# Splitting one weight load and reordering two value loads in a fused attention and SwiGLU kernel

## Chip, cores and metric

The kernel runs on one core of one Trainium2 chip. The metric is the device time of one execution in microseconds (us). A core has five engines that run beside each other and wait for one another by semaphores: PE (TensorE, the matmuls), DVE (VectorE), ACT (ScalarE), POOL (GpSimd) and SP (SyncE, which only starts transfers here). PEld is PE's weight load. Transfers started by POOL, by SP and by ACT share the core's 16 DMA engines.

## What is computed

Attention without a mask over 8 batches, 12 heads, 448 tokens and head size 64, then a SwiGLU block over all 3584 tokens. Inputs and output are float32; the kernel computes in float16 with float32 sums.

```python
scores = (q @ k.T) / sqrt(64)                  # per batch and head, 448 x 448
attn   = softmax(scores)
x      = (attn @ v) -> [3584, 768]             # heads side by side
out    = (silu(x @ w_gate) * (x @ w_val)) @ w_out   # 768 -> 1536 -> 768
```

## The kernel before

**Pairs.** Two heads form a pair; there are 48 pairs, numbered 0 to 47, six to a batch. `q` and `k` of a pair are loaded by POOL with a cast to float16 into `qkraw`, brought into the order for a transpose, and turned so that the head dimension lies on the partitions (`qkT`). From pair 11 on POOL copies them into `qk` (L237 and L260) and SP starts a DMA transpose in two halves (L239 and L243 from pair 12 on). PE multiplies keys by queries (`qk_quad`: L329 for a pair's own three chunks, L341 for a rest chunk, tile `s`), ACT takes the exponential into `E` (L349), and PE multiplies `E` by the values (`pv_*`, L420, tile `acc`). DVE normalizes into `xt` (L449 and L450). The rest chunk is shared: an even pair from 12 (QUAD) on and the odd one behind it put their last 64 keys of each head together, so L341 needs the `qkT` of both pairs.

**Values.** `load_v` asks for the values of a pair: one transfer below pair 12, two of 64 KB each (`load_keys`, L177) from pair 12 on. They land in `vraw`, and DVE copies them (`copy_v`, L218) into `vo`, which L420 reads.

**Weights.** `load_w` loads a quarter of the gate or value weights in two transfers, or one half (384 of the 768 output columns) of the output weights `wo` in one transfer (L231, 1152 KB in float16). The second half of the columns is `wo[1]`. `plain_out` multiplies 12 row blocks `fb` of `hts` by the 12 row blocks of `wo[oh]` in turn (L650, tile `op`). The differences of `wo` for later products (`out_sums`, L529 to L532) run on DVE and read both.

**Order.** Each engine executes its instructions in the order in which the program emits them (`manual_schedule`). The loop over `plan` emits one visit after another. In a visit stand, in this order: two or three chunks of scores, the opening of a value product (`pv_open`, `pv_rest`), the preparation of pairs `pr` whose first chunk is entered (`prep`, then `load_qk16` of pair `pr + 6`, then `load_v` of pair `pr + 3`), the rest of the value product with its normalization, `copy_v` of the pair that comes next, the weights that `wq` lists for `pr`, and a share of the feed-forward work (`run_o` for L650 with its DVE sums, `run_pair` for two gate and value blocks: L557, L584, L610, L616). So POOL's queue holds, around the change:

- entering pair 8: copies of pair 11, queries and keys of 14 (three transfers: one of queries, two of keys), `wo[1]`
- entering pair 9: copies of pairs 12 and 13, queries and keys of 15, values of 12
- entering pair 10: copies of pair 14, queries and keys of 16, values of 13
- entering pair 11: copies of pair 15, queries and keys of 17, values of 14
- entering pair 12: copies of pair 16, queries and keys of 18, values of 15, and so on

PSUM tiles that matter: `acc`, `vp` and `op` come from a pool of two banks (`ps_f`); `s` and `gp` from a pool of three double banks (`ps_s`). A matmul that starts a tile waits until the earlier tile in that bank has been read.

Of the kernel before, what the change touches and what calls it, by code (L numbers as in the profile page):

```python
# [18 lines left out]
GP = 3  # L19
# [13 lines left out]
QUAD = 12  # L33
# [31 lines left out]
def kernel(  # L65
# [10 lines left out]
    nc = tc.nc  # L76
# [6 lines left out]
    NFB = DF // 128  # L83
    NHP = H // 2
    NPAIR = B * NHP
# [3 lines left out]
    OH = DM // 2  # L89
# [47 lines left out]
    NH = NFB // 2  # L137
# [16 lines left out]
    wo = [wo_all[:, i] for i in range(2)]  # L154
# [17 lines left out]
    def load_keys(eng, dst, src, h0, n):  # L172
        for s in range(2):
            rows = bass.AP(
                src.tensor, (h0 * S + s * KR) * D, [[(2 * NC - 1) * D, 64], [S * D, n], [1, NC * D]]
            )
            eng.dma_start(dst[ts(s, 64)], rows)  # L177
# [8 lines left out]
    def load_qk16(pr, n=2):  # L186
        for t, src in ((0, q), (1, k)):
            if pr >= QUAD and t:
                if n == 1:
                    kd = rawslot(pr)[:, 1].rearrange("p (h x) -> p h x", h=2)  # L190
                else:
                    kd = raws_all[:, pr % RS // 2, 1].rearrange("p b (h x) -> p (b h) x", h=2)
                load_keys(nc.gpsimd, kd, k, 2 * pr, 2 * n)
                continue
            flat = src.rearrange("b h s d -> (b h) s d")[2 * pr : 2 * pr + 2 * n]
            if n == 1:
                dst = rawslot(pr)[0:P, t].rearrange("p (h x) -> p h x", h=2)
            else:
                dst = raws_all[0:P, pr % RS // 2, t].rearrange("p b (h x) -> p (b h) x", h=2)
            nc.gpsimd.dma_start(dst, flat.rearrange("h (p c) d -> p h (c d)", c=NC))  # L200
        for p in range(pr, pr + n):
            v4 = rawslot(p).rearrange("p t (h c d) -> p t h c d", h=2, c=NC)
            raw[p] = (v4[0:P, 0], v4[:, 1] if p >= QUAD else v4[0:P, 1])

    def load_v(pr, n=1):
        b, h = divmod(2 * pr, H)
        if pr >= QUAD:
            vd = vraw[:, ds(pr % VS, n)].rearrange("p r h c d -> p (r h) (c d)")
            load_keys(nc.gpsimd, vd, v, 2 * pr, 2 * n)
            return  # L210
        nc.gpsimd.dma_start(
            vraw[0:P, ds(pr % VS, n)].rearrange("p r h c d -> p (r h) (c d)"),
            v[b, h : h + 2 * n].rearrange("h (p c) d -> p h (c d)", c=NC),
        )
# [2 lines left out]
        m = 128 if pr >= QUAD else P  # L217
        nc.vector.tensor_copy(Vts[pr % NV][0:m, :, :, 0:D], vraw[0:m, pr % VS])  # L218

    def load_w(kind, i):  # L220
        if kind == "o":
            src = moe_w_out[:, ts(i, OH)].rearrange("(f p) m -> p f m", p=128)
            dst = wo[i]
        else:
            src = (moe_w_gate if kind == "g" else moe_w_val)[:, ts(i, DF // 4)].rearrange(
                "(t a p) m -> t p a m", p=128, t=2
            )
            for t in range(2):
                nc.gpsimd.dma_start(wgv[kind, i][:, ts(t, NCB // 2), :], src[t])
            return  # L230
        nc.gpsimd.dma_start(dst[:], src)  # L231

    def prep_quad(pr):
        rq, rk = raw[pr]
        qk16 = attp.tile([128, 2, NC, 2, D], FP16, tag="qk16", name="qk16", bufs=3)
        for dst, src in ((qk16[:, 0], rk), (qk16[0:P, 1], rq)):
            nc.gpsimd.tensor_copy(dst.rearrange("p c h d -> p h c d"), src)  # L237
        qkT[pr] = attp.tile([128, NC * 128 + S], FP16, tag="qkT", name="qkT", bufs=QB)
        nc.sync.dma_start_transpose(  # L239
            qkT[pr][:, 0 : NC * 128].rearrange("p (c q) -> p c q", q=128),  # L240
            qk16[:, 0].rearrange("p c h d -> p (c h d)"),
        )
        nc.sync.dma_start_transpose(  # L243
            qkT[pr][:, NC * 128 :].rearrange("p (c q) -> p c q", q=P),
            qk16[0:P, 1].rearrange("p c h d -> p (c h d)"),
        )

    def prep(pr):
        if pr >= QUAD:
            return prep_quad(pr)  # L250
        rq, rk = raw[pr]
        if pr == 0 or pr >= NPE:
            qk16 = attp.tile([128, 2, NC, 2, D], FP16, tag="qk16", name="qk16", bufs=3)[0:P]
            for t, src in enumerate((rq, rk)):
                dst = qk16[:, 1 - t].rearrange("p c h d -> p h c d")
                if pr == 0:
                    nc.vector.tensor_copy(dst[:, 0], src[:, 0])
                    nc.scalar.activation(dst[:, 1], src[:, 1], AF.Copy)
                else:
                    nc.gpsimd.tensor_copy(dst, src)  # L260
        qkT[pr] = attp.tile([128, 2 * S + D], FP16, tag="qkT", name="qkT", bufs=QB)
        if pr >= NPE:
            nc.sync.dma_start_transpose(
                qkT[pr][:, 0 : 2 * S].rearrange("p (c q) -> p c q", q=P),
                qk16.rearrange("p t c h d -> p (t c h d)"),
            )
            nc.sync.dma_start_transpose(
                qkT[pr][:, 2 * S :].rearrange("p (c q) -> p c q", c=1),
                qk16[0:D, 1, 0].rearrange("p h d -> p (h d)"),
            )  # L270
            return None

        def turn0():
            for t in range(2):
                tp = ps_s.tile([128, 2, 512], FP32, tag="s", name="tp")
                for c in range(NC):
                    for hx in range(2):
                        nc.tensor.matmul(
                            tp[ts(hx, 64), c // 2, ds(c % 2 * P, P)],
                            lhsT=qk16[:, 1 - t, c, hx],  # L280
                            rhs=ident[0:P, 0:P],
                            start=True,
                            stop=True,
                        )
                dst = qkT[pr][:, ts(1 - t, S)].rearrange("p (a x) -> p a x", a=2)
                copies = [nc.vector.tensor_copy(dst[:, 0], tp[:, 0, 0 : 2 * P])]
                if t == 0:
                    copies.append(nc.vector.tensor_copy(qkT[pr][:, 2 * S :], tp[:, 0, 0:D]))
                other = nc.scalar.activation(dst[:, 1], tp[:, 1, 0 : 2 * P], AF.Copy)
                for copy in copies:  # L290
                    tc.declare_no_dep(other.ins, copy.ins, reason="another bank, other columns")

        def turn():
            if pr < WIDE + 2:
                tp = ps_s.tile([128, 2, 1024], FP16, tag="s", name="tp")[:, 0]
            else:
                tp = ps_f.tile([128, 1024], FP16, tag="f", name="tp")
            for i in range(2 * NC + 1):
                t, c = (1 - i // NC, i % NC) if i < 2 * NC else (0, 0)
                for hx in range(2):  # L300
                    src = raw[pr][t][:, hx, c, :]
                    nc.tensor.transpose(tp[ts(hx, 64), ts(i, P)], src, ident[0:P, 0:P])  # L302
            nc.vector.tensor_copy(qkT[pr][:], tp[:, 0 : 2 * S + D])

        return turn if pr else turn0
# [585 lines left out]
    with tc.manual_schedule():  # L891
# [6 lines left out]
        for vo in Vts:  # L898
# [14 lines left out]

        wq = {
            0: [("qk", 6), ("g", 0), ("v", 0)],
            1: [("V", 2), ("qk", 8, 1), ("g", 1), ("v", 1)],
            3: [("qk", 9, 1), ("qk", 10), ("g", 2), ("v", 2)],
            4: [("g", 3), ("v", 3), ("qk", 12)],
            6: [("V", 3), ("o", 0)],
            8: [("o", 1)],  # L920
        }

        def emit(item):
            if item[0] == "qk":
                load_qk16(*item[1:])
            elif item[0] == "V":
                load_v(item[1] * GP, GP)
            else:
                load_w(*item)

# [233 lines left out]
        g = FIRST * NC  # L1164
# [36 lines left out]
        for x, (chunks, todo) in enumerate(plan):  # L1201
# [23 lines left out]
            for pr in entered:  # L1225
                lead = [pr + 3] if pr + 3 < QUAD else [pr + 3, pr + 4] if pr + 3 == QUAD else [pr + 4]
                for p in lead:
                    if NPE <= p < NPAIR:
                        prep(p)
                if 14 <= pr + LA < NPAIR:  # L1230
                    load_qk16(pr + LA, 1)
                if 12 <= pr + 3 < NPAIR:
                    load_v(pr + 3)
            for pr, c in chunks:
                if c == 2 and pr < NPE - 2:
# [13 lines left out]
            for pr in entered:  # L1249
                for w in wq.pop(pr, []):  # L1250
                    emit(w)
# [204 lines left out]
```

## Time and profile before

| | |
|---|---|
| median of 3 runs | 428.99 us (428.96 to 429.71) |
| profiled execution, its own time | 429.37 us |
| its span, first to last instruction | 427.6 us |
| mean granted TensorE clock | 0.998 |
| DVE busy | 270.1 us (63%) |
| ACT busy | 245.1 us (57%) |
| POOL busy | 232.3 us (54%) |
| transfers started by POOL | 24.56 MB |
| transfers started by SP | 24.47 MB |

Times in the timeline count from the start of the span. A line of it gives start, duration, engine, source line, operation, tiles (written first, read behind the arrow), the number of instructions merged into it and, in square brackets, how long the engine sat idle before it and what ended that. Starting a transfer takes POOL 0.6 to 1.0 us; the transfer then lands later, and the view of transfers tells after how long. A matmul's end is modelled, so neighbouring lines of PE overlap a little.

### The profile page before, as it was taken

The page shows a single profiled execution, that of the slowest core. Times are in us where ns is not written, and L with a number is a line of the kernel's source. Part 1 is how long each engine was busy: PE and PEld are TensorE (multiplying, and loading weights), DVE is VectorE, ACT ScalarE, POOL GpSimd, SP SyncE. Part 2 cuts the span into 40 slices and gives each one's busy share as a digit, 9 for nine tenths or more (in the row PEclk, how much of TensorE's full clock was granted, in tenths as well). Part 3 has the DMA queues.
Part 4 walks back from the last instruction along what each step waited for, and adds up shares of the span by engine and source line. Part 5 has one row for each costly group of instructions (what it writes and reads, how often), then busy time and mean ns, then how long its engine had stood idle before and what let it go on. Part 6 is the DMA issues. An engine that isn't in the chain of part 4 may idle for free.

```text
span 427.6 us, 11629 instructions
## 1 busy us (share of the span) xinstructions
PE 420.1 (98%) x4636; PEld 289.8 (68%) x4636; DVE 270.1 (63%) x643; ACT 245.1 (57%) x395; POOL 232.3 (54%) x353
## 2 busy tenths in 40 slices
PE   8999999999999999999999999999999999999996
PEld 3666656555556777747666677777888995555795
DVE  4666562676669665575545776667777765565663
ACT  6975667546656655546667546568655235545221
POOL 8655633999778683649653785935999000000000
PEclk9999999999999999999999999999999999999999
DMA  9999999999999999999989996823100331000125
GB/s 139 181 200 200 199 174 188 137 159 218 138 136 122 137 159 135 127 153 134 126 147 122 149 151 106 145 45 97 25 1 18 97 102 48 0 0 2 38 76 148
DMA packets 108951, 50.02 MB, mean 117 GB/s; under 512 B 60896, under 2 KB 105696, under 8 KB 108896
## 3 DMA queue, kind: packets, MB, share of 16 engines
q0 software_dynamic: 46800, 24.56, 49.6%
q1 hardware_dynamic: 61776, 24.47, 34.7%
q8 instruction: 36, 0.59, 0.6%
q10 hardware_dynamic: 320, 0.25, 0.2%
q14 instruction: 19, 0.16, 0.2%
HBM read 49.55 MB, written 11.01 MB: 142 GB/s over the span
## 4 chain that ended last, share of the span: by engine, by line
PE 89%; DVE 3%; ACT 3%; DMA 2%; issue 1%; POOL 1%; SPq 0%; ACTq 0%; DVEq 0%; POOLq 0%
PE og L679 17%; PE gp L557 17%; PE vp L557 12%; PE un L802 10%; PE ub L802 8%; PE acc L420 8%; PE s L329 5%; PE op L650 3%; PE acc L385 2%; PE s L359 2%; DMA qkT<-qk 1%; ACT E L367 1%; PE s L341 1%; PE tp L302 1%; DVE t L610 1%; PE wp L163 1%
## 5 line engine op out<-in xcount | busy, mean ns | idle before, releaser
L349 ACT ACTIVATE E<-s 128x896 f16<-128x896 f32 x126 | 106.6, 918 | 40.5 <-PE s L329 28.5
L557 PE MATMUL gp<-X,wg 128*128 128x384 f16 (+1 forms) x360 | 73.9, 347 | 0.0
L237 POOL COPY qk<-qkraw 128x512 f16<-128x512 f16 x72 | 45.2, 668 | 51.4 <-DMA qkT<-qk 50.6
L557 PE MATMUL vp<-X,wv 128*128 128x384 f16 (+3 forms) x360 | 66.7, 321 | 0.2
L610 DVE SCALAR_TENSOR_TENSOR t<-sg,gp 128x384 f32<-128x384 f32 (+1 forms) x60 | 36.3, 607 | 41.4 <-ACT sg L584 41.2
L557 PEld LDWEIGHTS <-wv 128*128 128x128 f16 x462 | 43.7, 98 | 26.2 <-DVE xt L450 0.5
L557 PEld LDWEIGHTS <-wg 128*128 128x128 f16 x360 | 32.8, 98 | 26.3 <-issue 2.1
L177 POOL DMA_DIRECT2D vraw<-in_v_dram x72 | 43.8, 627 | 11.5 <-DVE hts L616 7.6
L584 ACT ACTIVATE sg<-gp 128x384 f32<-128x384 f32 (+1 forms) x60 | 32.1, 537 | 28.1 <-PE gp L557 27.4
L177 POOL DMA_DIRECT2D qkraw<-in_k_dram x70 | 42.3, 616 | 6.8 <-DMA wo<-in_moe_w_out_dram 5.1
L367 ACT ACTIVATE E<-s 112x896 f16<-112x896 f32 x48 | 40.6, 917 | 8.4 <-PE s L359 8.3
L420 PEld LDWEIGHTS <-E 128*128 128x128 f16 (+1 forms) x1152 | 37.4, 96 | 11.2 <-issue 4.7
L679 PEld LDWEIGHTS <-hts 128*128 128x128 f16 x528 | 44.1, 98 | 0.3
L420 PE MATMUL acc<-vo,E 128*128 128x65 f16 (+1 forms) x1152 | 42.3, 192 | 0.9 <-DVE X L492 0.3
L616 DVE SCALAR_TENSOR_TENSOR hts<-t,vp 128x384 f16<-128x384 f32 (+3 forms) x60 | 32.5, 541 | 5.4 <-PE vp L557 1.9
L704 ACT ACTIVATE osb<-og 128x384 f32<-128x384 f32 x21 | 10.3, 491 | 38.1 <-PE og L679 38.1
L450 DVE TENSOR_TENSOR xt<-acc,R 128x256 f16<-128x256 f32 x72 | 30.6, 425 | 2.5
L200 POOL DMA_DIRECT2D qkraw<-in_q_dram x43 | 29.3, 681 | 4.0 <-DMA vraw<-in_v_dram 0.9
L329 PE MATMUL s<-qkT 64*128 64x448 f16 x216 | 30.2, 354 | 0.2
L679 PE MATMUL og<-wo,hts 128*128 128x192 f16 x264 | 29.0, 246 | 0.0
L679 PEld LDWEIGHTS <-hsum 128*128 128x128 f16 x300 | 25.5, 98 | 1.2 <-DVE og L728 0.3
L449 DVE RECIPROCAL R<-acc 128x4 f32<-128x4 f32 x72 | 12.7, 177 | 18.6 <-PE acc L420 18.4
(181 smaller groups left out, 713.8 us busy)
## 6 DMA issues: line engine op xcount, KB each, us to landing
vraw<-in_v_dram POOLq DMA_DIRECT2D x72, 64.0 KB, 4.5
qkraw<-in_q_dram POOLq DMA_DIRECT2D x39, 112.0 KB, 4.4
qkraw<-in_k_dram POOLq DMA_DIRECT2D x68, 64.0 KB, 4.4
wg<-in_moe_w_gate_dram POOLq DMA_DIRECT2D x8, 288.0 KB, 10.1
wv<-in_moe_w_val_dram POOLq DMA_DIRECT2D x8, 288.0 KB, 10.7
wo<-in_moe_w_out_dram POOLq DMA_DIRECT2D x2, 1152.0 KB, 19.5
out_dram<-osb SPq DMA_DIRECT2D x7, 288.0 KB, 3.8
out_dram<-osb SPq DMA_DIRECT2D x6, 336.0 KB, 3.2
```

What stands on the lines that cost most here:

```text
L177: eng.dma_start(dst[ts(s, 64)], rows)
L237: nc.gpsimd.tensor_copy(dst.rearrange("p c h d -> p h c d"), src)
L329: nc.tensor.matmul(s[:, hx, 0:S], lhsT=t[ts(hx, 64), ts(c + low(pr, hx), 128)], rhs=t[ts(hx, 64), ds(NC * 128, S)], start=True, stop=True,)
L349: nc.scalar.activation(e[:, 0 : 2 * S].rearrange("p (h q) -> p h q", h=2), s[:, :, 0:S], AF.Exp, scale=sm_scale)
L367: nc.scalar.activation(e[:, :, 0:S], s[0:P, :, 0:S], AF.Exp, scale=sm_scale)
L420: nc.tensor.matmul(acc[:, ts(j, D + 1)], lhsT=e[rows, ds(hx * S + j * 128, 128)], rhs=Vts[pr % NV][rows, hx, col, 0 : D + 1], start=first, ...
L557: nc.tensor.matmul(dst[:, 0:w], lhsT=wslice(kind, self.fb, cb), rhs=X[kk][:, cb, ds(c0 + lo, w)], start=(cb == 0), stop=(cb == NCB - 1),)
L584: self.readers = [nc.scalar.activation(self.sg[:, 0:n], gp[:, 0:n], AF.Tanh, scale=0.5)]
L610: nc.vector.scalar_tensor_tensor(self.t1[:, 0:n], self.sg[:, 0:n], 1.0, self.gp[:, 0:n], ALU.add, ALU.mult)
L616: nc.vector.scalar_tensor_tensor(self.hts[:, self.fb, ds(lo, w)], self.t1[:, ds(lo, w)], 0.5 * HS, vp[:, 0:w], ALU.mult, ALU.mult)
L679: nc.tensor.matmul(dst, lhsT=lhs(n), rhs=rhs(n), start=first and n == 0, stop=n == NH - 1, skip_group_check=True)
L802: mm = nc.tensor.matmul(dst, lhsT=lhs[:, n], rhs=rhs[:, n], start=first and n == 0, stop=n == NK - 1, skip_group_check=True,)
```

## The change

`wo[1]` is loaded in two transfers of six row blocks each instead of one of twelve. The first stays where it was; the second follows the values of pair 12, and both now stand ahead of queries and keys of pair 15. The values of pair 13 move from behind queries and keys of pair 16 to behind the copies of pair 15, ahead of queries and keys of pair 17. POOL's queue becomes:

- entering pair 8: copies of 11, queries and keys of 14, first part of `wo[1]`
- entering pair 9: copies of 12 and 13, values of 12, second part of `wo[1]`, queries and keys of 15
- entering pair 10: copies of 14, queries and keys of 16
- entering pair 11: copies of 15, values of 13, queries and keys of 17, values of 14
- entering pair 12 and later: as before

```diff
-    def load_w(kind, i):
+    def load_w(kind, i, part=slice(0, NFB)):
         if kind == "o":
-            src = moe_w_out[:, ts(i, OH)].rearrange("(f p) m -> p f m", p=128)
-            dst = wo[i]
+            src = moe_w_out[:, ts(i, OH)].rearrange("(f p) m -> p f m", p=128)[:, part]
+            dst = wo[i][:, part]
...
-        nc.gpsimd.dma_start(dst[:], src)
+        nc.gpsimd.dma_start(dst, src)
...
-            1: [("V", 2), ("qk", 8, 1), ("g", 1), ("v", 1)],
+            1: [("V", 6, GP), ("qk", 8, 1), ("g", 1), ("v", 1)],
...
-            6: [("V", 3), ("o", 0)],
-            8: [("o", 1)],
+            6: [("V", 9, GP), ("o", 0)],
+            8: [("o", 1, slice(0, NH))],
...
-                load_v(item[1] * GP, GP)
+                load_v(*item[1:])
...
+                if pr == QUAD - 3:
+                    load_v(QUAD)
+                    load_w("o", 1, slice(NH, NFB))
+                if pr == QUAD - 1:
+                    load_v(QUAD + 1)
                 if 14 <= pr + LA < NPAIR:
                     load_qk16(pr + LA, 1)
-                if 12 <= pr + 3 < NPAIR:
+                if QUAD - 1 <= pr < NPAIR - 3:
                     load_v(pr + 3)
```

The edits of the entries `V` only write the same two loads with other arguments. The number of bytes loaded stays the same; the number of transfers grows by one.

## Prediction

> **What bounds the kernel now.** I read the page first: PE is busy nearly all of the span, so an edit of loads can only move the little that PE waits.
>
> ```profile
> PE 420.1 (98%) x4636; PEld 289.8 (68%) x4636; DVE 270.1 (63%) x643; ACT 245.1 (57%) x395; POOL 232.3 (54%) x353
> ```
>
> Then the waits of 66 to 84 us, where the moved transfers are used:
>
> ```profile
> POOL qkraw L177 <- DMA wo<-in_moe_w_out_dram: 5.1, 1, 5.1
> ...
> DVE vo L218 <- DMA vraw<-in_v_dram: 1.6, 1, 1.6
> ...
> PEld L420 <- DVE vo L218: 0.6, 1, 0.6
> ...
> PE acc L420 <- DVE X L492: 0.3, 1, 0.3
> ```
>
> The values of pair 12 are late for their copy, and PE waits for the copy. In PE's timeline the first matmul of pair 12's values starts at 76.89 and the other 31 at 77.35, while the scores ahead of it (six in 0.68 us from 75.93) end at 76.61: PE loses 77.35 - 76.61, about **0.7 us**, once for the copy and once for the DVE cast (L492) queued behind it. The chain of waits from 76 to 92 us names a second loss:
>
> ```profile
> 77.98 5.96 DMA qkT<-qk
> 83.94 0.04 issue
> 83.99 0.38 PE s L341 x3
> 84.37 0.84 PE acc L420 x24
> ```
>
> The four L341 last 0.80 us here against 0.38 at 71.94, since the second needs pair 15's transpose, landed at 83.98: **0.42 us**. Elsewhere near the change PE waits for nothing. The most that can be won is 0.7 + 0.4 = 1.1 us.
>
> **How the loads queue.** In POOL's timeline the holes say when it may issue:
>
> ```profile
> 64.14 0.60 POOL L177 DMA_DIRECT2D vraw<-in_v_dram  x1 [7.25 <-DVE hts L616]
> ...
> 73.53 0.59 POOL L177 DMA_DIRECT2D qkraw<-in_k_dram  x1 [5.06 <-DMA wo<-in_moe_w_out_dram]
> 74.88 1.18 POOL L177 DMA_DIRECT2D vraw<-in_v_dram  x2 [0.75 <-DVE xt L406]
> 76.05 1.25 POOL L237 COPY qk<-qkraw 128x512 f16<-128x512 f16 x2
> 77.25 0.66 POOL L200 DMA_DIRECT2D qkraw<-in_q_dram  x1
> ```
>
> Each late issue starts 0.2 to 0.6 us behind the landing of the transfer eight places ahead of it: the values of 12 (64.14) behind `wo[0]` (issued 46.55, 17.1 us to land: 63.65), the last keys of 16 (73.53) behind `wo[1]` (51.23 + 22.0 = 73.2), the values of 13 (74.88) behind the queries of 15 (55.01 + 19.3 = 74.3). I take it as a rule of this program: eight POOL transfers outstanding, and they land in order of issue. Landings behind `wo[1]`: queries of 15 at 74.3, keys of 15 at 74.76 and 75.28, values of 12 at 76.14 and 76.28, queries of 16 at 76.7, keys at 77.1 and 77.4, values of 13 at 77.8 and 78.2.
>
> **The change, part by part.** Times are on the profiled execution's clock.
>
> *Values of 12 ahead.* They are issued at 55.0, as POOL then is free (eight places ahead stand transfers of before 52.7). Ahead of them lies only the first part of `wo[1]`. `wo[1]` took from 65.9 (landing of the keys of 14) to 73.2, 7.3 us; half is 3.65, so it lands at 69.6, and the values 1.0 later (76.28 - 75.28), at **70.6**. Their copy then runs behind DVE's L406, at 74.8, and L492 right after PE's part: the 0.7 us go.
>
> *Second part of `wo[1]`.* It lands at 73.2 + 1.0 = 74.2. The first `op` to read it starts at 73.71, and reaches row block 6 after half of its 1.96 us: 74.69. Cover 0.5 us, so nothing; without that cover, what it is late.
>
> *Queries and keys of 15 behind it.* They may be issued from 63.65 on, the third at about 65.9, which pushes pair 14's copies from 66.11 to some 66.5. Their transposes wait anyway for pair 13's, landed at 70.0. In the landing order the same bytes stand ahead of the last keys of 15 as stood ahead of the last values of 12, so they land at about **76.3** in place of 75.28. POOL, which reached pair 15's copies at 76.05, now starts them at 76.3 + 0.15 = 76.45. The transposes move by 0.4; between 0 (they wait for DMA anyway) and +0.4 at L341, and then the second loss stays. It is no new bound if the values of 13 are later still.
>
> *Values of 13 behind those copies.* Copies plus handing over took 1.2 us (76.05 to 77.25), so the two issues stand at **77.65 and 78.25** instead of 74.88 and 75.46. This is the costly edit. The transfers into `vraw` of this stretch took at least 2.7 us to land, and the two of pair 14, issued at 79.08, 5.1. The spread has a cause in the view of transfers from 79 to 83 us:
>
> ```profile
> DMA  9486699999999999999999990101117400079999
> GB/s 67 21 36 36 72 138 164 128 133 154 169 185 205 220 243 382 223 192 174 120 51 33 26 10 0 10 5 15 10 10 13 8 13 18 18 100 195 160 189 210
> ...
> q8 instruction: 1, 0.02, 1.5%
> ```
>
> From about 80.9 to 82.5 hardly a byte moves. Such a gap follows the 16 KB instruction fetch (here at 80.5) also at 61.2, 109, 121 and 132 us, each within 1.5 us (hardly the one at 70.0). The page counts 36 such fetches for PE's 2 x 4636 instructions, some 258 each, so I take it that the gap goes with PE's place in its program. The queries of 17, which now hold this place in the queue, landed at 82.55, right behind it. With 2.7 us the values of 13 land at 80.95, in the gap; so they land at its end: 82.6 if it stays, 81.9 if PE, 0.7 us ahead, brings it along. I take 82.3, between them. The copy, at 80.39 before, then starts at about 82.5: **late by d = 2.1 us**.
>
> *What hangs on the copy.* DVE takes its instructions in order, and from the copy on it has no hole for 7 us:
>
> ```profile
> 80.39 0.68 DVE L218 COPY vo<-vraw 128x512 f16<-128x512 f16 x1
> 80.99 0.96 DVE L529 TENSOR_TENSOR E<-wo 128x768 f16<-128x768 f16 x1
> ...
> 84.95 0.96 DVE L531 TENSOR_TENSOR E<-wo 128x768 f16<-128x768 f16 x1
> 85.83 0.17 DVE L449 RECIPROCAL R<-acc 128x4 f32<-128x4 f32 x1
> ...
> 88.46 0.69 DVE L610 SCALAR_TENSOR_TENSOR t<-sg,gp 128x512 f32<-128x512 f32 x1 [0.61 <-ACT sg L584]
> ...
> 90.44 0.42 DVE L616 SCALAR_TENSOR_TENSOR hts<-t,vp 128x256 f16<-128x256 f32 x1 [0.23 <-PE vp L557]
> ```
>
> Seven differences of `wo`, pair 13's normalization, pair 14's copy and the gate products follow. The only slack until L616 at 90.44 is 0.61 + 0.23 = 0.84 us. That L616 (to 90.86) frees the bank that pair 14's `acc` starts in at 90.91, with nothing to spare. So PE there is late by d - 0.84 = 2.1 - 0.84 = **1.26 us**; what it won at 77 and 84 us it gives back in waiting for DVE. Later visits win nothing back, since PE is the bound. Pair 16's copies move from 80.25 to some 81.9; its first scores stand at 97.2 and its transposes landed at 86.4: no cost.
>
> **Sum.** -0.7 (values of 12), 0 to -0.4 (transpose of 15), both swallowed, then +1.26: 429.37 + 1.3 = 430.7 by the profiled execution. That one lies 0.4 above the median, so beside the median it is 428.99 + 1.3 = **430.3**. With d from 1.8 (landing right behind a gap moved forward) to 2.5 (resuming 0.3 us later) the cost is 0.96 to 1.66, 429.9 to 430.7.
>
> **Rivals.**
> 1. *The values of 13 come before the gap.* For it: 80.95 misses it by little, and were the keys of 15 earlier by 0.5 us, all would be. Then d is at most 0.84 and costs nothing, but DVE, in order from 80.4 on, lets PE keep at most 0.84 - d. With the shortest landing, 2.7 us, d is 0.7; with keys 0.5 us earlier besides it is 0.2: the time is 429.0 - 0.1 to 429.0 - 0.6. Against it: the queries of 17, issued at 77.25, still landed behind the gap, at 82.55. 428.4 to 429.1, likeliest 428.9. Chance 25%. Beside it stands a rule of the Trainium skill ("DMA: Bandwidth & Descriptors", section "Anatomy of one DMA — SWDGE (gpsimd) path"): a transfer takes about 2.0 us plus its bytes at 436 GB/s, as an estimate 2.15 us for 64 KB, so the values of 13 would land at 80.4, ahead of the gap, and the time would be 428.3. The trace's shortest, 2.7, does not bear it out.
> 2. *Not slower: both losses go.* It needs keys of 15 landed by 75.3 as before, so copies at 75.4, values of 13 issued by 77.2 and landed by 79.9: the copy is at its old place or ahead, and pair 15's transposes, issued 0.6 us earlier, finish before the gap. It decides at d = 0. Price -0.9 to -1.1: 428.0. The view of landings speaks against it: 1.0 us of values now lies ahead of those keys. Chance 8%.
> 3. *Worse: the gap also catches pair 15's second transpose whole* (it started at 80.0; 0.4 us later it hardly begins), which then needs the 2.0 us that pair 16's took from its first packets, at 83.25, to landing. L341 and the values of 13 go to some 84.8, d to 3: +2.2, 431.2. Chance 10%.
>
> That the values of 12 stay late, so that the edit misses its aim, needs the first part of `wo[1]` to land 4 us later than half of 7.3 us: I give it nothing of its own.
>
> **How the numbers follow.** My forecast holds 57%, the rivals 25, 8 and 10%. 0.2% is 0.86 us, about what a measurement of this kernel can tell from no change. Slower by more: rival 3 and most of the forecast's 0.96 to 1.66, less 9% for its low end: 10 + 48 = 58%. Within: 25 + 9 + 1 = 35%. Faster by more: 7%. The range reaches from rival 1's low end, 428.4, to rival 3's 431.3; left out are rival 2 and what lies past 3.
>
> **What would show it.** Right: pair 12's copy with no wait and both L420 lines one; POOL issuing the values of 13 between two copies near 77.7; DVE idle ahead of pair 13's copy for over 1 us, "DVE vo L218 <- DMA vraw" among the waits; PE then waiting at `vp` or `acc` around 88 to 91 us behind DVE. Wrong: pair 13's copy starts by 81.2; the gap is not there, or not behind the fetch; or `op` waits at 74.7.

## The result, and the profile after

| | before | after |
|---|---|---|
| median of 22 runs each, side by side | 429.33 us (428.84 to 432.27) | 430.8 us (430.06 to 431.7) |
| ratio, 95% interval | | 1.003 [1.0019, 1.0041] |
| the profiled execution's own time | 429.37 us | 431.42 us |
| its span | 427.6 us | 429.6 us |
| mean granted TensorE clock | 0.998 | 1.0 |

The changed kernel is slower by 1.5 us by the medians and 1.3 us by the ratio, whose interval is 0.8 to 1.8 us. The forecast was +1.3. The profiled execution lies 0.6 above its median, so sizes read from it are somewhat large.

First the waits of the profile after, from 60 to 100 us (total, times, longest):

```profile
DVE vo L218 <- DMA vraw<-in_v_dram: 2.4, 1, 2.4
...
PE vp L557 <- DVE xt L450: 1.8, 1, 1.8
...
PE s L329 <- DMA qkT<-qk: 0.6, 1, 0.6
PE acc L420 <- DVE vo L218: 0.5, 1, 0.5
...
PE op L650 <- DMA wo<-in_moe_w_out_dram: 0.2, 1, 0.2
```

DVE now waits 2.4 us for values, as it waited 1.6 us before, but one pair later: for those of pair 13. PE's two old waits are gone and four others stand there, 0.16 + 0.60 + 0.53 + 1.75 = 3.0 us. POOL's timeline shows where the values of 13 come from:

```profile
76.57 1.17 POOL L237 COPY qk<-qkraw 128x512 f16<-128x512 f16 x2 [5.46 <-DMA qkraw<-in_k_dram]
77.68 1.19 POOL L177 DMA_DIRECT2D vraw<-in_v_dram  x2
```

The copies of pair 15 waited for its keys until 76.57, and the values of 13 could be issued only behind them. DVE's timeline shows the use:

```profile
73.90 0.28 DVE L218 COPY vo<-vraw 128x512 f16<-128x512 f16 x1
...
82.35 0.85 DVE L218 COPY vo<-vraw 128x512 f16<-128x512 f16 x1 [2.41 <-DMA vraw<-in_v_dram]
...
85.95 1.64 DVE L529 TENSOR_TENSOR E<-wo 128x768 f16<-128x768 f16 x1
...
88.85 0.42 DVE L450 TENSOR_TENSOR xt<-acc,R 128x256 f16<-128x256 f32 x1
```

Pair 12's copy (73.90) has no wait: the aim of the edit is met. Pair 13's copy starts at 82.35 in place of 80.39, and the chain behind it ends later still. PE's timeline:

```profile
74.22 1.14 PE L650 MATMUL op<-wo,hts 128*128 128x384 f16 x6 [0.16 <-DMA wo<-in_moe_w_out_dram]
...
76.61 0.37 PE L329 MATMUL s<-qkT 64*128 64x448 f16 x2 [0.60 <-DMA qkT<-qk]
76.80 1.14 PE L420 MATMUL acc<-vo,E 64*128 64x65 f16 x32
...
83.26 0.30 PE L420 MATMUL acc<-vo,E 64*128 64x65 f16 x8 [0.53 <-DVE vo L218]
83.49 0.67 PE L341 MATMUL s<-qkT 64*64 64x448 f16 x4
...
89.33 1.47 PE L557 MATMUL vp<-X,wv 128*128 128x512 f16 x6 [1.75 <-DVE xt L450]
```

The 32 matmuls at 76.80 are one line again, so the loss at pair 12's values is gone. What it cost stands at 89.33. The first `vp` doesn't read pair 13's output: it starts in the PSUM bank in which pair 13's `acc` stood, and PE waits until L450 has read that bank. In before the two places that matter are these:

```profile
87.63 1.46 PE L557 MATMUL vp<-X,wv 128*128 128x512 f16 x6
...
90.91 1.12 PE L420 MATMUL acc<-vo,E 64*128 64x65 f16 x32
```

Set against before, row by row: in this execution PE was 0.79 us ahead when it entered the stretch (the `op` of 24 matmuls starts at 64.25, in before at 65.04). It was 0.21 ahead at the gate product (84.83; in before 85.04), then 1.70 behind at `vp` (89.33; 87.63) and 1.96 behind at pair 14's `acc` (92.87; 90.91). The span is 2.0 longer. So the loss lies between 65 and 93 us: 0.6 until the gate product, where the lead shrinks, 1.9 at that one `vp`, and 0.3 behind it.

### The profile page after: what moved, and what is told of

It reads as the page before. It is cut to its first block, busy times and chain, and to the rows that moved or that the text cites. A ratio compares the mean times of both kernels' runs of the same rounds, so it can differ in the third digit from the quotient of the medians.

```text
span 429.6 us, 11631 instructions
## 1 busy us (share of the span) xinstructions
PE 419.6 (98%) x4636; PEld 289.8 (67%) x4636; DVE 270.1 (63%) x643; ACT 244.9 (57%) x395; POOL 231.4 (54%) x354
## 4 chain that ended last, share of the span: by engine, by line
PE 80%; DMA 12%; DVE 3%; ACT 2%; issue 1%; POOL 1%; SPq 0%; ACTq 0%; DVEq 0%; POOLq 0%
PE og L679 17%; PE gp L557 14%; PE un L802 10%; PE vp L557 9%; PE acc L420 8%; PE ub L802 8%; PE s L329 5%; DMA qkraw<-in_k_dram 4%; DMA wv<-in_moe_w_val_dram 3%; PE op L650 3%; DMA qkraw<-in_q_dram 2%; DMA qkT<-qk 2%; PE s L359 1%; PE acc L385 1%; PE s L341 1%; ACT E L349 1%
## 5 line engine op out<-in xcount | busy, mean ns | idle before, releaser
L237 POOL COPY qk<-qkraw 128x512 f16<-128x512 f16 x72 | 44.0, 655 | 60.4 <-DMA qkT<-qk 51.4
L616 DVE SCALAR_TENSOR_TENSOR hts<-t,vp 128x384 f16<-128x384 f32 (+3 forms) x60 | 32.4, 541 | 5.7 <-PE vp L557 1.6
L450 DVE TENSOR_TENSOR xt<-acc,R 128x256 f16<-128x256 f32 x72 | 30.6, 425 | 2.5
```

The source lines that it names most:

```text
L616: nc.vector.scalar_tensor_tensor(self.hts[:, self.fb, ds(lo, w)], self.t1[:, ds(lo, w)], 0.5 * HS, vp[:, 0:w], ALU.mult, ALU.mult)
```

## The experiments

My theory was that of the prediction: the values of 13, issued behind copies that the heavier queue has pushed back, come too late, and PE pays through DVE. The rivals: the split itself costs (keys and transposes of 15 later), and the gap in the transfers behind PE's instruction fetch is what makes the values late. Where an experiment says "before" or "after", it is that kernel with only the edit shown. Times are medians beside that of the kernel before on the same chip, and the ratio stands with its 95% interval.

### Each part alone

The split with the values of 12 ahead, without the move of 13 (an edit of the changed kernel, run twice):

```diff
-                if pr == QUAD - 1:
-                    load_v(QUAD + 1)
...
-                if QUAD - 1 <= pr < NPAIR - 3:
+                if QUAD - 2 <= pr < NPAIR - 3:
```

> The change without its last part: the output weights are split and the values of pair 12 stand between the two, but the values of pair 13 are asked for behind queries and keys of 16, ahead of the copies of pair 15, as before. Theory (the late values of 13, through DVE's queue, are the whole cost): they land by about 79, their copy stands at its old place, PE does not wait at vp, and the 0.7 us at pair 12's values are won, less what pair 14's transpose is late (0 to 0.6 us): 0 to 0.7 us below the kernel before, 1.3 to 2 below the changed one. Rival (splitting the weights and pushing queries and keys of 15 back is the cost): 1.0 to 1.5 us above the kernel before, as the changed kernel is.

> The split with the values of 13 at their old place once more, for a second profile: the first one's span was only 0.1 us above the kernel before, its median 0.9. If pair 14's transpose is the cost, PE waits for it between 0.5 and 1.4 us here, the more the earlier PE arrives (at 65.08 at the double op block in the first profile, at 64.25 in that of the changed kernel), and the transpose lands 7 us or more behind pair 13's. If not, the wait is below 0.5 us and another one, at L341 or behind DVE, is over 0.5.

Measured: 430.14 beside 429.22, ratio 1.0028 [1.0004, 1.0052], and 430.14 beside 429.53, 1.0012 [0.9998, 1.0026]. My theory had 0 to 0.7 us below before and its rival 1.0 to 1.5 above; the medians are 0.9 and 0.6 above, between the two. The move of 13 alone, on the kernel before:

```diff
+                if pr == QUAD - 1:
+                    load_v(QUAD + 1)
...
-                if 12 <= pr + 3 < NPAIR:
+                if 12 <= pr + 3 < NPAIR and pr + 3 != QUAD + 1:
```

> The last part of the change alone: weights and values of pair 12 as before, only the values of pair 13 moved behind the copies of pair 15. The keys of 15 then land at 75.3 as before, so the copies start at 75.45 and the values of 13 are issued at 76.7 and 77.3, a microsecond ahead of the changed kernel. Theory (late values act by what DVE can't hide, 0.84 us): with 4.0 us to land they come at 81.3, 0.9 us late, and cost 0 to 0.3 us, while pair 15's transpose, 0.6 us earlier, gives back up to 0.4: between 0.4 below and 0.4 above the kernel before; both parts of the change are needed for its cost. Rival A (the move alone is the cost): 1.0 to 1.5 above. Rival B (the move is harmless and the weights cost): 0.4 below to 0, and DVE's copy of 13 without a wait.

Measured: 429.35 beside 429.22, 1.0003 [0.9989, 1.0016]: no difference. There the copies of 15 start at 75.01, the values of 13 are issued at 76.12 and land by 79.7, earlier than the 81.3 that I had expected, and pair 13's copy has no wait:

```profile
79.99 0.44 DVE L218 COPY vo<-vraw 128x512 f16<-128x512 f16 x1
```

So asking for those values behind the copies costs nothing measurable by itself. In the changed kernel, where the first part makes the copies start 1.5 us later, the same place is late. Pair 15's second transpose landed at 81.7 here and L341 has no wait, so the 0.42 us there was won; but PE had come 0.8 us earlier than in before and lost about as much more in waiting for the values of 12.

The first part alone wins nothing, though its profile has no wait at pair 12's values. PE's timeline of the first run:

```profile
76.99 0.36 PE L329 MATMUL s<-qkT 64*128 64x448 f16 x2 [0.48 <-DMA qkT<-qk]
77.18 1.14 PE L420 MATMUL acc<-vo,E 64*128 64x65 f16 x32
...
84.03 0.38 PE L341 MATMUL s<-qkT 64*64 64x448 f16 x3 [0.25 <-DMA qkT<-qk]
...
90.96 1.12 PE L420 MATMUL acc<-vo,E 64*128 64x65 f16 x32
```

Two other things are late in place of the values: pair 14's second transpose (0.48) and pair 15's (0.25; the rest of that wait is hidden behind the first of the four L341). Pair 14's `acc` starts at 90.96, in before at 90.91. The second run was to tell whether pair 14's transpose is the cost. In its profile PE does not wait for that transpose at all, but 0.52 us for pair 15's, so pair 14's transpose is not the steady cost.

### Where the win at pair 12 goes

The first part without its split: the values of 12 behind the whole of `wo[1]`, but ahead of queries and keys of 15. Then the same with the values of 13 behind the copies of 15. In a third kernel the whole of `wo[1]` goes behind the values of 12. All three are edits of the kernel before; the first one's is:

```diff
+                if pr == QUAD - 3:
+                    load_v(QUAD)
...
-                if 12 <= pr + 3 < NPAIR:
+                if QUAD < pr + 3 < NPAIR:
```

> The values of 12 behind the unsplit output weights, ahead of queries and keys of 15; values of 13 at their old place. Theory I (the cost of the split run is pair 14's transpose, pushed by the issue of the last keys of 15): the copies of 14 keep their place at 66.1, the transpose lands at 76.1, the values of 12 land at 74.2 and PE loses nothing at them; the last keys of 15 land at 76.3 as with the split: 0 to 0.7 us below the kernel before. Rival (the cost is the keys of 15 landing a microsecond later, through pair 15's transpose): 0.5 to 1.2 above the kernel before, as the split run, with PE waiting at L341.

> The run before this one with the values of 13 moved behind the copies of pair 15, as in the change: the changed order without the split. Theory (late values of 13 cost by DVE's queue, as the changed kernel's profile shows): keys of 15 at 76.3, values of 13 issued at 77.7 and 78.3, copied at about 82, PE waits 1 to 1.8 us at vp for DVE's L450: 1.0 to 1.8 us above the run before this one. Rival (what the changed kernel lost is pair 14's transpose and DVE's wait is hidden in most executions): within 0.4 us of the run before this one.

> No split: the values of 12 stand ahead of the whole second half of the output weights, both behind the copies of pairs 12 and 13; values of 13 at their old place. In the kernels with the split, pair 14's transpose landed 7.0 to 7.3 us behind pair 13's, in those without it 5.6 to 6.5. Theory I (its issue: the third transfer of queries and keys of 15 holds POOL until 66.5, and the transpose lands 7.7 to 8.3 us after each issue): here the third may go at 65.3, the copies of 14 start at 66.1 and the transpose lands at its old place, 76.1 to 76.3. Theory II (its packets alternate with the larger ones of the weights, which now last a microsecond longer): it lands at 76.9 as with the split. The weights land at 74.2, so op waits some 0.5 us at 73.7 in both. Time by I: 0.3 us below to 0.4 above the kernel before; by II: 0.5 to 1.2 above.

Measured: unsplit 429.89 beside 429.53, 1.0011 [0.9998, 1.0025]; with the values of 13 late 431.20, 1.0038 [1.0023, 1.0052]; the whole behind the values 429.70, 1.0008 [0.9993, 1.0023]. The first was forecast 0 to 0.7 us below before by the theory and 0.5 to 1.2 above by its rival; its 0.4 above lies between, but PE waits at L341, as the rival said. The unsplit kernel's PE timeline shows where the win goes:

```profile
76.75 1.14 PE L420 MATMUL acc<-vo,E 64*128 64x65 f16 x32
...
84.00 0.38 PE L341 MATMUL s<-qkT 64*64 64x448 f16 x3 [0.64 <-DMA qkT<-qk]
```

PE reaches pair 12's matmuls without the 0.7 us loss. It comes to L341 at 82.98, 0.58 us earlier than in before (83.56), and goes on at 84.00, when pair 15's second transpose has landed, as it had in before (83.94). What was won is given back seven microseconds on: the transpose is the later bound.

The first two of these kernels differ only in the place of the values of 13, so they give the price of that edit without the split: 431.20 - 429.89 = **1.3 us**, on one chip (1.2 by the ratios, whose intervals hardly overlap). The profile of the second has pair 13's copy at 83.89 after 2.59 us of waiting, and `vp` waiting 0.97; that execution took 433.03 us, 1.8 more than the median, and its loads were late already at 75 us, so only the kind of wait is to be read from it.

The third kernel gave one more answer. With the whole of `wo[1]` behind the values, `op` waits 1.24 us for it (in the changed kernel 0.16), so the split does what it says. And pair 14's transposes, issued at their old time (the second at 67.95), landed by 76.3, as the theory of their issue had it.

### Later still

The values of 13 behind the queries and keys of 17, weights as before, and the changed kernel again beside it:

```diff
                     load_qk16(pr + LA, 1)
-                if 12 <= pr + 3 < NPAIR:
+                if pr == QUAD - 1:
+                    load_v(QUAD + 1)
+                if 12 <= pr + 3 < NPAIR and pr + 3 != QUAD + 1:
```

> Weights and values of 12 as before the change; only the values of 13 moved, behind queries and keys of 17, so that they are issued at about 78.5 and 79.1, as late as in the changed kernel (77.7 and 78.3), without the keys of 15 being pushed. Theory (late values of 13 are a cost by themselves, by what exceeds DVE's 0.84 us): the copy starts at about 82.2, DVE idle for some 2 us ahead of it, PE waits 1 to 1.6 us behind DVE's L450: 0.8 to 1.6 us above the kernel before. Rival (it takes the pushed weights and keys besides): within 0.4 us of it.

> The changed kernel once more, for a second profile. If the first is typical, DVE waits over 2 us for the values of 13 and PE 1.2 to 1.8 us at vp for L450, and pair 15's transpose lands at 83.7 to 84.3, so that nothing is left of what was won at pair 12's values. If the first was an odd one, the wait at vp is below 0.6 and another one makes up the 1.3 to 1.5 us.

Measured: 432.13 beside 429.41 (six runs), 1.0063 [1.0043, 1.0083], with pair 13's copy at 85.16 and `vp` waiting 1.64. This is more than the 0.8 to 1.6 us expected. The profiled execution took 432.73, and all its loads were some 1.5 us late already at 75 us (`op` waits 0.78 there), so its rows do not give the size; but even the shortest run, 431.48, is 2.1 us above before's median. A late issue of these values is thus a cost without the pushed weights and keys too. The changed kernel again: 430.93, 1.0038 [1.0023, 1.0053]. Its profiled execution, at 430.91, is a typical one. DVE's timeline, then PE's:

```profile
81.52 0.29 DVE L218 COPY vo<-vraw 128x512 f16<-128x512 f16 x1 [1.59 <-DMA vraw<-in_v_dram]
```

```profile
88.69 1.47 PE L557 MATMUL vp<-X,wv 128*128 128x512 f16 x6 [1.04 <-DVE xt L450]
...
92.31 1.12 PE L420 MATMUL acc<-vo,E 64*128 64x65 f16 x32
```

Here the copy is 1.1 us later than in before (80.39) and `vp` waits 1.04. From the `op` of 24 matmuls to pair 14's `acc` there lie 92.31 - 64.82 = 27.49 us, in before 90.91 - 65.04 = 25.87: +1.6, close to the measured 1.5.

### Is the gap behind the fetch the cause?

Sixty short warm-up matmuls in place of seven long ones put 106 more PE instructions (weight loads and matmuls) ahead of everything, so that PE's instruction fetches fall elsewhere. First on the kernel before, then on the changed one:

```diff
-        dummy(7)
+        wp = ps_f.tile([128, 512], FP32, tag="f", name="wp")
+        for _ in range(60):
+            nc.tensor.matmul(wp[:, 0:128], lhsT=warm[:], rhs=warm[:], start=True, stop=True)
```

> The kernel before with 60 short warm-up matmuls (128 columns) in place of 7 long ones at the start: 106 more PE instructions ahead of everything, about the same PE time. Theory (the gap in the traffic follows the fetch of PE's instructions, so it goes with the place in PE's program): the fetch of 80.5 comes at 77 to 77.8, the gap behind it at 77.5 to 79.5, none at 81 to 82.4, and pair 15's second transpose lands at about 82.5, so that L341 no longer waits. Rival (the gap has another cause, such as what the other engines do there): it stays at 81 to 82.5. Time within 0.8 us of the kernel before in both cases.

> The changed kernel with 60 short warm-up matmuls in place of 7 long ones at the start, which moved PE's instruction fetch of about 80 us to about 76 and the next to 87 when done to the kernel before (0.4 us above it by itself). Theory (the gap behind the fetch is what makes the values of 13 take 4 us to land): no gap between 78 and 82, the values of 13 land 2.7 to 3.3 us behind their issue at 77.7 and 78.3, so at 81 to 81.5, and PE's wait at vp is 0 to 0.6 us: 0.4 to 1.0 us above the kernel before. Rival (they are slow because of the transposes and the transfers beside them): 3.8 us or more to land, a wait of 1 us or more at vp, and 1.6 to 2.0 above.

Measured: on before 429.59 beside 429.22, 1.0016 [1.0005, 1.0027]; on after 431.2 beside 429.73, 1.0035 [1.0022, 1.0047]. The view of transfers from 79 to 83 us, first of the changed kernel (without the longer warm-up), then of before with it:

```profile
DMA  9909999400029999999999999999999809999999
GB/s 97 18 0 31 33 44 46 10 8 10 10 44 208 179 159 179 200 195 139 169 159 200 179 185 210 256 274 282 253 207 74 38 18 131 182 140 143 154 149 195
```

```profile
DMA  3002873769999999999999999999899996999999
```

Each digit, and each number, is 0.1 us. With the fetch moved, the gap that before had from 81 to 82.5 is not there; one stood at 68.7 to 69.4, behind a fetch at 67.7. So the gap does follow the fetch.

What the gap adds to the cost of the change is less clear. In the changed kernel the fetch came at 78.5 and the gap lay earlier and was shorter than I took it to be (at most 46 GB/s from 79.1 to 80.1, 1.0 us), and the values of 13 landed at 81.4 and 82.3, behind its end. With the fetch moved they land 3.2 and 3.0 us after their issue in place of 3.8 and 4.1. But the gap then struck the weights (68.2 to 69.0): the first part of `wo[1]` landed at 71.1 in place of 69.6, the copies of 15 came at 77.49, the values of 13 were issued 0.9 us later, and pair 13's copy stood at 82.20. PE's wait at `vp` is 0.68. I had expected 0.4 to 1.0 us above before, and by the rival 1.6 to 2.0; the medians say 1.5, in neither range. The longer warm-up by itself costs 0.4 of that, so on top of it the change costs some 1.1 us, where it cost 1.5; the intervals don't tell these two apart. The late issue thus costs without a gap at the landing, and a share of the gap is neither shown nor excluded.

### Can DVE's order save it?

The changed kernel with pair 13's copy moved behind four of the seven differences of `wo`, so that the differences run while the values are on their way:

```diff
+        held = [None, 0]
...
+                    held[1] += 1
+                    if held[0] is not None and held[1] == 4:
+                        copy_v(held[0])
+                        held[0] = None
...
-                if p0 not in early:
+                if p0 == QUAD + 1:
+                    held[:] = [p0, 0]
+                elif p0 not in early:
```

> The changed kernel with DVE's copy of the values of 13 behind four of the seven differences of the output weights instead of ahead of all; all transfers as in the change. Theory (DVE's order is what makes the late landing cost): the four fill DVE's idle time from 79.9 to 82.2, the copy starts as late as before, but pair 13's normalization ends before PE needs its bank, so the wait of 1.75 us at vp goes: 1.2 to 1.9 us below the changed kernel, 0.6 below to 0.2 above the kernel before. Rival (PE's waits for the transfers themselves, pair 14's transpose and the values of 13, are the cost): within 0.4 us of the changed kernel.

Measured: 430.25 beside 429.22, 1.0028 [1.0013, 1.0042]. The wait at `vp` is gone, so that wait was DVE's chain. But of the 1.5 us only some 0.5 came back by the medians, and 0.1 by the ratios, whose intervals don't tell the two kernels apart. I had expected 1.2 to 1.9:

```profile
77.10 0.36 PE L329 MATMUL s<-qkT 64*128 64x448 f16 x2 [0.73 <-DMA qkT<-qk]
...
84.06 0.30 PE L420 MATMUL acc<-vo,E 64*128 64x65 f16 x8 [0.84 <-DVE vo L218]
```

PE now waits 0.84 for the values themselves, at pair 13's `acc`, and 0.73 for pair 14's transpose.

The last try was for a faster kernel: before with the values of 13 moved, and with DVE's cast of L492 ahead of pair 12's copy, so that PE waits there only once.

```diff
-                if p0 not in early:
+                if p0 not in early and p0 != QUAD:
...
+            last_copy = [p0 for p0 in vcopies.get(x, []) if p0 == QUAD]
...
+            for p0 in last_copy:
+                copy_v(p0)
```

> The run with only the values of 13 moved, and in it DVE's cast L492 ahead of the copy of the values of 12. PE's second stop there (0.26 us for the cast behind the copy) goes, the first (the landing of the values) stays: 0.2 to 0.5 us below that run, so 0 to 0.5 below the kernel before. If PE's stop is the landing alone, no difference to that run.

Measured: 429.52 beside 429.41, 1.0001 [0.9991, 1.001], not the 0 to 0.5 us below before that I had expected. Pair 12's matmuls are one line at 76.58; but the second transfer of the values of 13, issued behind the first at 76.19 as in the other kernel, landed only at 81.4 (there at 79.7), and `vp` waits 0.65. In this execution hardly a byte moved from 79.7 to 81.2, behind PE's fetch at 79.5: here the gap did catch that transfer. No kernel here beats the one before.

## Why the prediction was right, and where it wasn't

**Values of 12 ahead: right.** No wait at their copy (73.90), one line of 32 matmuls. **Second part of `wo[1]`: right,** landing at 74.2 as forecast; its cover was short by 0.16 us in the profile taken, which I had put among the signs of being wrong; in the second profile `op` doesn't wait.

**Keys of 15, copies, issue of the values of 13: right.** Forecast 76.45 and 77.65, measured 76.57 and 77.68 (76.32 and 77.43 in the second profile).

**Landing of the values of 13: right in number, wrong in reason.** Forecast 82.3 with the copy at 82.5; measured 82.33 with the copy at 82.35, and 81.50 in the typical execution. I had them land at the end of a gap of 1.6 us that ends at 81.9 to 82.6. In the profile taken PE's fetch came at 78.5, not at 79.8 to 80.5, the gap ended at 80.1, and the values landed 1.3 and 2.2 us behind it; in the second profile no stretch of 79 to 83 us was empty; and with the fetch moved they still took 3.0 us. What made them late is their issue at 77.68 and some 4 us to land (2.7 to 2.9 in before, issued at 74.88; why it is longer is not shown). That 82.3 was hit is partly luck. Behind the copies of pair 15, these two transfers took 3.0 to 4.7 us to land over the profiles. The Trainium skill's estimate ("DMA: Bandwidth & Descriptors", section "Anatomy of one DMA — SWDGE (gpsimd) path", 2.15 us for 64 KB) isn't borne out by this.

**What hangs on the copy: right in mechanism, wrong in place and terms.** I had the bound at L616 and pair 14's `acc`, with 0.84 us of slack. Among the signs I had named `vp` too, but I gave it no price. The bound came there, earlier, since `vp` needs the bank of pair 13's `acc`: in before DVE had read that bank at 86.45 (86.03 + 0.42) for a `vp` at 87.63, a slack of 1.18. Against that, DVE's chain from the copy to the normalization, 80.39 to 85.83 or 5.44 us in before, took 6.29 in after and 6.48 in the typical execution, which I had not counted (why it varies is not shown). So: 1.96 + 0.85 - 1.18 = 1.6 us in the profile taken, where PE's `vp` moved by 1.70; in the typical one 1.13 + 1.04 - 1.18 = 1.0, its wait 1.04. The errors partly offset each other: the slack was larger than I had it, and the chain longer.

**The rivals: none came.** Pair 13's copy was late by 1.13 and 1.96 us, too late for the first two, and pair 15's second transpose landed at 83.7 and 83.8, not at 84.8 as in the third (priced at 431.2 there, written as 431.3 in the range).

**The failed step: "Their transposes wait anyway", and with it the -0.7 and -0.4 in the sum.** Pair 14's second transpose lands some 8 us after its issue: 68.03 to 76.1 in before, 68.27 to 76.5 in after, 67.95 to 76.3 in the kernel with that issue at its old time. In before PE came to it too late to notice. Once the wait at pair 12 is gone, PE comes 0.35 to 0.73 us too early in four of the six profiles with the split. And pair 15's, landed at 83.6 to 84.1 in all six (in before at 83.9), takes back the rest where PE comes early enough. So the values of 12 were not worth 0.7 us with the values of 13 in their old place: the first part alone stands 0.6 to 0.9 us *above* before by the medians, with intervals that reach from -0.1 to 2.2 us. That the sum came out at +1.3 beside the measured 1.5 rests on these two being read as swallowed, not on their being right. It also hides how the cost is made up. The sum has all of it from the values of 13; by the medians the first part brings 0.6 to 0.9 us, and the move of 13 on top of it another 0.7 (430.8 - 430.14), while without the split the move brings 1.3.

**What isn't settled.** The 0.6 to 0.9 us of the first part alone. Its profiles put pair 14's `acc` where before has it (90.96 and 91.08 beside 90.91). A part is visible later. In the kernels that load the values of 12 behind `wo[1]` or its first part and ahead of the keys of 15, the first difference of `wo` (L529) gets one more semaphore instruction on DVE. In all seven profiles in which that is the only one added, DVE's product L616 at 112 to 116 us starts some 0.4 us late, and PE with it; in the six without it and in the one with two more (the copy behind four differences) it doesn't. For the unsplit kernel, the row of that instruction in the view of line L529 (how often, ns, and where), and PE's timeline:

```profile
L529 DVEq EVENT_SEMAPHORE  x1: 21/21/21, 79.6 to 79.6; - x1
```

```profile
113.06 1.11 PE L420 MATMUL acc<-vo,E 64*128 64x65 f16 x31 [0.45 <-DVE hts L616]
```

That kernel's span ends 0.3 us later than before's, and its median stands 0.36 above. Why L616 is late is not shown: the trace puts its wait down to PE's L341 (111.71 to 112.09), for which L616 does not wait in before, and its place in DVE's program may matter, which wasn't tried. The rest of what the first part costs is not located.

## What to carry to other kernels

A load that is late is one place in a queue. Before moving another ahead of it, look up what the next bound of the same stretch is (here the transposes landing at 76.1 and 83.9): a win ahead of it is given back there. And when two edits touch one queue, price the second with the first's delay in it: the move of the values of 13 cost nothing measurable by itself, and 1.3 us behind keys that had been pushed back.

## What the runs showed of the hardware that I had not expected

- The stop of nearly all transfers for about 1 us follows PE's instruction fetch when the fetch is moved: from 81 to 82.5 us behind a fetch at 80.5 in before, from 68.7 to 69.4 behind one at 67.7 with 106 more instructions. It does not follow every fetch: hardly behind that kernel's next one, at 76.4, nor behind the one at 70.2 in before.
- DVE's difference of two 128x768 halves of `wo` takes 0.55 us, and 1.64 at 85.95 in after, where POOL copies from 85.91 to 87.17. The Trainium skill ("SBUF — State Buffer", section "Who interferes with whom") says that a DVE instruction with two SBUF inputs contends with a GpSimd instruction that reads SBUF; the row agrees. It is not the whole of it: the 0.96 at 84.18 in the same profile has no copy of POOL beside it. The whole chain of DVE, from pair 13's copy to its normalization, took 5.05 to 6.48 us over the profiles with the same order of work.
- Two 64 KB transfers, issued at the same place (from 76.12 and 76.19 on), were both there at 79.7 in one profile and at 81.4 in another, in which the gap behind a fetch lay between: the landing behind the same queue varied by 1.8 us, more than all that was at stake here.
